# Decoding 64-bit weights: the sign kept by a parametric ReLU instead of a mask

## The chip, the cores and the metric

The kernel runs on one core of a Trainium2 chip. A core has five engines with a queue each: TensorE (matmuls, PE in the profile), VectorE (DVE), ScalarE (ACT), GpSimd (POOL) and SyncE (SP), which here sends the DMAs. Each engine works through its queue in order and waits for the others by semaphores. The time is that of one execution on the device in microseconds; before, the median of three runs is 1021.5 us.

## The reference

Attention with 32 global and 512 local positions for 8 batches of 8 heads, and behind it a feed-forward layer whose activation is h·cos(h):

```
s_g = scale * q_g @ k_all.T ; out_g = softmax(s_g) @ v_all
s_l = concat(scale * q_l @ k_g.T, where(|i-j| <= 32, scale * q_l @ k_l.T, -1e9))
out_l = softmax(s_l) @ concat(v_g, v_l)
x = concat(out_g, out_l) as (4352, 512)
h = x @ w_in            # w_in  (512, 2048), float64
out = (h * cos(h)) @ w_out   # w_out (2048, 512), float64
```

The weights come as 64-bit floats, and the kernel receives them as 64-bit words.

## The kernel before

**Staging.** Attention runs per batch b (8) and pair of heads p (4); names like `kl_0_3` or `t_0_2_1` carry b, p and, for scores, the query block. Each operand is split into a high and a low 16-bit float, and products are made of three matmuls. A pair goes: load q and k (`qkr`), maximum and scale (`qm`, `d_qk`, `pm_qk`, `qs`), split (`qa`, `kl`), copies within SBUF by DMA that rearrange halves (`kh`, `qa`, `kl`: L547 to L552), scores (`ps`, `t`), exponentials (L446), probabilities as `planes`, their transposes `pt`, and the product with v (`acc`), which becomes `xh` and `xl`. The feed-forward layer goes through chunks c of 256 rows and steps j: `ph` = x·w_in (L919), `u` and `w` (cosine by the Sin table), `gf`, its split `gh` and `gl`, and `po` = g·w_out (L975 to L977).

**Weights.** w_in comes in 8 slices `wi0` to `wi7` of 128 x 1024 words, w_out in 16 slices `wo0` to `wo15` of 128 x 512. A slice is loaded, its maximum found (L288), and later decoded and split into two 16-bit floats (`split_w`: the high part a cast on ScalarE, L281; the low part a subtraction on GpSimd, L231). w_out is loaded once for its maximum (`raw_wm`) and once more to be decoded (L416, L244). The slots are few: `wi4` and `wi5` go into the slots that `wi0` and `wi1` leave when they are decoded, and the shifted w_out words `z` have one buffer, so that the next shift waits for the cast and the subtraction of the one before.

**A decode.** The high 32-bit word of a 64-bit float, read as a 32-bit float, is scaled on ScalarE by a power of two so that a left shift by three drops the sign and the two exponent bits that are then of no use (L262, L237: `y`). VectorE makes `lo`, the bits to be put in: the top three bits of the low word with a sticky one (L263, on 16-bit words), and the sign bit in the upper half (L266, on 16-bit words). VectorE then shifts `y` and puts `lo` in (L268).

**Order.** The code gives each step a slot and a phase, and from them a priority; a scheduler with a time model of its own then sets the order in each engine's queue. A step that gets shorter in that model can move others in all queues. Attention of batches 0 and 1 and all weight decodes lie at the start of the program; later batches run beside the feed-forward layer.

Of the kernel before, what the change touches and what calls it, by code (L numbers as in the profile page):

```python
# [10 lines left out]
F32 = mybir.dt.float32  # L11
U16 = mybir.dt.uint16
I64 = mybir.dt.int64
U32 = mybir.dt.uint32
AF = mybir.ActivationFunctionType
ALU = mybir.AluOpType
# [48 lines left out]
YE = [1, 1]  # L65
# [72 lines left out]
def body(tc, qk, v, wi, wo, mask, out):  # L138
    nc = tc.nc
# [4 lines left out]
    with ExitStack() as ctx:  # L144
# [88 lines left out]
        def scaled(engine, o, a, s):  # L233
            if engine == 0:
                nc.vector.tensor_scalar(o, a, s, None, op0=ALU.mult)
            elif engine == 1:
                nc.scalar.activation(o, a, AF.Identity, scale=s)  # L237
            else:
                sb = bass.AP(tensor=s.tensor, offset=s.offset, ap=[s.ap[0]] + [(0, n) for _, n in a.ap[1:]])
                nc.gpsimd.tensor_tensor(o, a, sb, op=ALU.mult)  # L240
# [6 lines left out]
        def decode(raw, s, name, wo=0, inplace=False):  # L247

            rf, rh = raw.bitcast(F32), raw.bitcast(U16)
            n = raw.shape[-1]
            if wo:
                y = w2.tile([P, n], F32, tag="wy", name=f"y_{name}")
                lo = w2.tile([P, n], U32, tag="wlo", name=f"lo_{name}", bufs=1)
            else:
                y = w2.tile([P, n], F32, tag="raw", name=f"y_{name}")
                lo = w1.tile([P, n], U32, tag="wl1", name=f"lo_{name}")  # L260
            lh = lo.bitcast(U16)
            scaled(YE[wo], y, rf[:, 1::2], s)  # L262
            nc.vector.tensor_scalar(  # L263
                lh[:, 0::2], rh[:, 1::4], 13, 1, op0=ALU.logical_shift_right, op1=ALU.bitwise_or
            )
            nc.vector.tensor_scalar(lh[:, 1::2], rh[:, 3::4], 0x8000, None, op0=ALU.bitwise_and)  # L266
            z = w2.tile([P, n], F32, tag="wfo", name=f"z_{name}", bufs=1) if wo and not inplace else y
            zins[name] = nc.vector.scalar_tensor_tensor(  # L268
                z.bitcast(U32), y.bitcast(U32), 3, lo,
                op0=ALU.logical_shift_left, op1=ALU.bitwise_or,  # L270
            ).ins
            return z
# [78 lines left out]
        def w_in_piece(k):  # L351
            kc, c = k // 2, slice(k % 2 * 1024, k % 2 * 1024 + 1024)
            z = decode(wfs.pop(("raw", k)), wfs["s", kc], f"wi{k}")
            split_w(wi_h[:, kc, c], wi_l[:, kc, c], z)
# [63 lines left out]
        def w_out_piece(j):  # L418

            if j == 0:  # L420
                zs = [decode(slot_of(k), wsc, f"wo{k}", 1, True) for k in range(2)]
                for k in range(2):
                    split_w(wo_h[:, k], wo_l[:, k], zs[k], k < WLV)
            elif j > 1:
                raw = slot_of(j) if j < 8 else load_raw(wo[j * P : (j + 1) * P, :], f"wo{j}")
                split_w(wo_h[:, j], wo_l[:, j], decode(raw, wsc, f"wo{j}", 1), j % 4 < WLV)
# [687 lines left out]
        for c in range(NC + 1):  # L1114
            at(NS * c, -11, chunk_scales, c)
            for j in range(NS):
                s = NS * c + j
# [91 lines left out]
```

## Time and profile before

| | before |
|---|---|
| time, median of three runs (lowest, highest) | 1021.5 us (1018.31, 1022.91) |
| profiled execution, span from the first to the last instruction | 1016.1 us |
| mean granted clock of TensorE | 0.975 |
| busy: TensorE | 880.3 us (87%) |
| busy: VectorE | 712.2 us (70%), 1811 instructions |
| busy: ScalarE | 718.5 us (71%) |
| busy: GpSimd | 461.4 us (45%) |
| moved by DMA | 120.19 MB |

For the profiled execution the profile gives the span alone; it lies below the lowest of the three timed runs, which also hold what lies around the span. Busy shares are means over the whole program. The start, where weights are decoded, and the rest have different limits and are read apart below. DMA shares are the mean busy share of the core's 16 DMA engines.

### The profile page before, as it was taken

The page shows a single profiled execution, that of the slowest core. Times are in us where ns is not written, and L with a number is a line of the kernel's source. Part 1 is how long each engine was busy: PE and PEld are TensorE (multiplying, and loading weights), DVE is VectorE, ACT ScalarE, POOL GpSimd, SP SyncE. Part 2 cuts the span into 40 slices and gives each one's busy share as a digit, 9 for nine tenths or more (in the row PEclk, how much of TensorE's full clock was granted, in tenths as well). Part 3 has the DMA queues.
Part 4 walks back from the last instruction along what each step waited for, and adds up shares of the span by engine and source line. Part 5 has one row for each costly group of instructions (what it writes and reads, how often), then busy time and mean ns, then how long its engine had stood idle before and what let it go on. Part 6 is the DMA issues. An engine that isn't in the chain of part 4 may idle for free.

```text
span 1016.1 us, 21123 instructions
## 1 busy us (share of the span) xinstructions
PE 880.3 (87%) x7947; PEld 603.6 (59%) x7947; DVE 712.2 (70%) x1811; ACT 718.5 (71%) x1469; POOL 461.4 (45%) x492
## 2 busy tenths in 40 slices
PE   1245697789899998999899999998989999999996
PEld 0133565456566666566567666666666667666663
DVE  5999878995878777777787878777776865432231
ACT  5788888986678777776777767876877876534341
POOL 3696478894233333343334333432423343444442
PEclk9997899899999999999999999999999999999998
DMA  9797155766454545456554553636446452000000
GB/s 358 283 281 277 15 155 146 169 162 149 109 108 104 102 139 111 101 105 164 104 113 105 141 127 77 129 78 160 88 109 106 109 84 62 16 21 22 1 21 21
DMA packets 165823, 120.19 MB, mean 118 GB/s; under 512 B 143065, under 2 KB 143065, under 8 KB 163673
## 3 DMA queue, kind: packets, MB, share of 16 engines
q1 hardware_dynamic: 165720, 118.85, 46.8%
q8 instruction: 62, 1.02, 0.4%
q14 instruction: 41, 0.33, 0.1%
HBM read 56.00 MB, written 8.91 MB: 64 GB/s over the span
## 4 chain that ended last, share of the span: by engine, by line
PE 29%; DVE 29%; DMA 16%; ACT 14%; issue 7%; POOL 4%; SPq 1%; ACTq 0%; DVEq 0%; POOLq 0%
PE ph L919 12%; DMA qkr<-qk 9%; PE po L975 5%; PE po L977 5%; PE po L976 5%; DVE planes L705 5%; DVE t L623 4%; DMA vr<-v 4%; ACT planes L702 3%; DVE u L942 3%; DVE kl L538 3%; ACT L446 3%; DVE qm L497 2%; ACT t L446 2%; POOL w L954 2%
## 5 line engine op out<-in xcount | busy, mean ns | idle before, releaser
L919 PE MATMUL ph<-xh,wi_h 128*128 128x256 f16 x1024 | 280.8, 275 | 13.7 <-DVE gf L956 13.7
L919 PE MATMUL ph<-xh,wi_l 128*128 128x256 f16 x1024 | 281.4, 275 | 0.0
L919 PE MATMUL ph<-xl,wi_h 128*128 128x256 f16 x1024 | 281.3, 275 | 0.0
L961 POOL TENSOR_TENSOR gl<-gf,gh 128x512 f16<-128x512 f32 x136 | 166.4, 1229 | 235.7 <-ACT gh L960 235.7
L954 POOL TENSOR_TENSOR w<-w 128x512 f32<-128x512 f32 x136 | 142.5, 1051 | 249.0 <-ACT w L446 249.0
L919 PEld LDWEIGHTS <-wi_h 128*128 128x128 f16 x2176 | 211.0, 98 | 58.5 <-issue 20.4
L975 PE MATMUL po<-wo_h,gh 128*128 128x512 f16 x544 | 206.4, 381 | 17.5 <-DVE o L983 17.5
L976 PE MATMUL po<-wo_l,gh 128*128 128x512 f16 x544 | 207.1, 381 | 2.1 <-POOL wo_l L231 2.1
L977 PE MATMUL po<-wo_h,gl 128*128 128x512 f16 x544 | 206.1, 380 | 0.3 <-POOL gl L961 0.3
L446 ACT ACTIVATE w<-u,ca 128x512 f32<-128x512 f32 x136 | 97.7, 721 | 108.9 <-DVE u L942 108.4
L942 DVE SCALAR_TENSOR_TENSOR u<-u,cm,ph 128x512 f32<-128x512 f32 x136 | 100.6, 741 | 88.1 <-ACT u L941 88.1
L446 ACT ACTIVATE t<-t,mn 128x192 f32<-128x192 f32 (+1 forms) x256 | 117.0, 458 | 48.8 <-DVE mn L623 48.1
L956 DVE SCALAR_TENSOR_TENSOR gf<-w,ph 128x512 f32<-128x512 f32 x136 | 92.6, 681 | 57.3 <-POOL w L954 57.1
L960 ACT CAST gh<-gf 128x512 f16<-128x512 f32 x136 | 83.1, 611 | 67.6 <-DVE gf L956 66.7
L919 PEld LDWEIGHTS <-wi_l 128*128 128x128 f16 x1088 | 107.3, 99 | 14.6 <-issue 1.2
L623 DVE CUSTOM_DVE_ANT_0 t<-ps,msk,al 128x192 f32<-128x192 f32 (+1 forms) x256 | 99.2, 425 | 7.0 <-PE ps L607 6.8
L941 ACT ACTIVATE u<-ph,cm 128x512 f32<-128x512 f32 x136 | 92.0, 677 | 13.3 <-PE ph L919 13.2
L705 DVE SCALAR_TENSOR_TENSOR planes<-t,sm,planes 128x192 f16<-128x192 f32 (+1 forms) x200 | 87.7, 487 | 10.8 <-ACT planes L702 10.8
L976 PEld LDWEIGHTS <-gh 128*128 128x128 f16 x544 | 53.3, 98 | 69.3 <-issue 20.8
L977 PEld LDWEIGHTS <-gl 128*128 128x128 f16 x544 | 53.4, 98 | 67.1 <-issue 3.2
L975 PEld LDWEIGHTS <-gh 128*128 128x128 f16 x544 | 53.2, 98 | 49.8 <-issue 0.9
L702 ACT ACTIVATE planes<-t,sm 128x192 f16<-128x192 f32 (+1 forms) x200 | 75.6, 454 | 0.0
(184 smaller groups left out, 1415.0 us busy)
## 6 DMA issues: line engine op xcount, KB each, us to landing
qkr<-qk SPq DMA_DIRECT2D x29, 608.0 KB, 4.9
vr<-v SPq DMA_DIRECT2D x8, 1280.0 KB, 8.4
kh<-qa SPq DMA_DIRECT2D x62, 152.0 KB, 2.6
out<-o SPq DMA_DIRECT2D x34, 256.0 KB, 3.2
raw_wm<-wo SPq DMA_DIRECT2D x16, 512.0 KB, 7.8
qa<-kl SPq DMA_DIRECT2D x31, 152.0 KB, 3.9
kl<-kl SPq DMA_DIRECT2D x31, 152.0 KB, 4.4
wo_h<-wi SPq DMA_DIRECT2D x4, 1024.0 KB, 6.9
```

What stands on the lines that cost most here:

```text
L446: ins = nc.scalar.activation(*a, **k).ins
L623: nc.vector.tensor_tensor_reduce(t[:, h], pt[:, h], msk[:, MOFF[i] : MOFF[i] + w], al, 3.0e38, ALU.add, ALU.min, mn[:, h : h + 1],)
L702: nc.scalar.activation(hi, t[:, h], AF.Identity, scale=r)
L705: nc.vector.scalar_tensor_tensor(lo, t[:, h], r, hi, op0=ALU.mult, op1=ALU.subtract)
L919: nc.tensor.matmul(ph[:, a], w[:, kc, f], x[:, kc, q], start=first and ip == 0, stop=last and ip == 2, skip_group_check=True,)
L942: nc.vector.scalar_tensor_tensor(u, u, m, ph, op0=ALU.subtract, op1=ALU.subtract)
L954: nc.gpsimd.tensor_tensor(w, w, w, op=ALU.mult)
L956: nc.vector.scalar_tensor_tensor(gf, w, 0.5, st.pop(("ph", c, j)).rearrange("p a b -> p (a b)"), op0=ALU.subtract, op1=ALU.mult,)
L961: nc.gpsimd.tensor_tensor(gl, gf, gh, op=ALU.subtract)
L975: nc.tensor.matmul(po[k], gh[:, q], wo_h[:, f], start=(f == 0), stop=False)
L976: nc.tensor.matmul(po[k], gh[:, q], wo_l[:, f], start=False, stop=False)
L977: nc.tensor.matmul(po[k], gl[:, q], wo_h[:, f], start=False, stop=(f == NJ - 1))
```

## The change

ScalarE's scaling becomes a Prelu with the same scale and a slope of 2^32 for negative values. A negative word thereby gets 32 more in its exponent field, and the left shift by three carries that bit, the sixth of the exponent, into the place of the sign. So `lo` has no sign to hold: one VectorE instruction on whole 32-bit words makes it, and the mask is gone.

```
-            rf, rh = raw.bitcast(F32), raw.bitcast(U16)
+            rf = raw.bitcast(F32)
...
-            lh = lo.bitcast(U16)
-            scaled(YE[wo], y, rf[:, 1::2], s)
+            nc.scalar.activation(y, rf[:, 1::2], AF.Prelu, scale=s, alpha=2.0**32)
             nc.vector.tensor_scalar(
-                lh[:, 0::2], rh[:, 1::4], 13, 1, op0=ALU.logical_shift_right, op1=ALU.bitwise_or
-            )
-            nc.vector.tensor_scalar(lh[:, 1::2], rh[:, 3::4], 0x8000, None, op0=ALU.bitwise_and)
+                lo, raw.bitcast(U32)[:, 0::2], 29, 1, op0=ALU.logical_shift_right, op1=ALU.bitwise_or
+            )
```

Each of the 24 decodes loses one VectorE instruction (1813 become 1789); the counts on the other engines stay, with 58 loads of an activation table in both. In the new kernel all lines behind the edit have numbers lower by two, so that its L266 is the old L268, and its L262 is the new instruction. The scheduler also sets another order in the early part of every queue: the last 1294 instructions on VectorE, 890 on ScalarE, 13307 on TensorE, 257 on GpSimd and 258 on SyncE stand as before.

The first place is VectorE at the second pair of w_in slices (`y_wi0` is the shift of slice 0, `lo_wi2` the bits of slice 2, `ws3_2` the maximum of slice 4, `gt` the global scores, L288 before and L286 now the maximum). Before:

```order
L268 SCALAR_TENSOR_TENSOR y_wi1_242<-y_wi1_242,lo_wi1_243 128x1024
L263 TENSOR_SCALAR lo_wi2_361<-raw_wi2_186 128x1024
L266 TENSOR_SCALAR lo_wi2_361<-raw_wi2_186 128x1024
L815 ISA gt_0_0_309,gmn_0_0_310<-gps_0_0_0_300,zero_74,gal_0_0_311 128x288
L815 ISA gmn_0_0_310 128x1
L263 TENSOR_SCALAR lo_wi3_440<-raw_wi3_188 128x1024
L266 TENSOR_SCALAR lo_wi3_440<-raw_wi3_188 128x1024
L623 ISA t_0_1_0_386,mn_0_1_0_387<-ps_0_1_0_381,msk_73,al_0_1_162 128x192
```

Now:

```order
L266 SCALAR_TENSOR_TENSOR y_wi1_241<-y_wi1_241,lo_wi1_242 128x1024
L262 TENSOR_SCALAR lo_wi2_359<-raw_wi2_185 128x1024
L343 TENSOR_SCALAR wm43_1_351<-wim_107 128x1
L262 TENSOR_SCALAR lo_wi3_437<-raw_wi3_187 128x1024
L301 TENSOR_SCALAR ws_1_350<-wm43_1_351 128x1
L196 TENSOR_SCALAR wie_108<-wm43_1_351 128x1
L302 TENSOR_SCALAR ws_1_350<-ws_1_350 128x1
L309 TENSOR_SCALAR pw_i_90<-wie_108 128x1
L286 TENSOR_REDUCE ws3_2_424<-wo_h_88 128x1
L310 TENSOR_SCALAR pw_i_90<-pw_i_90 128x1
L813 ISA gt_0_0_307,gmn_0_0_308<-gps_0_0_0_298,zero_74,gal_0_0_309 128x288
```

Two instructions of the pair are gone, and the maximum of slice 4 stands ahead of the scores, which it followed before.

The second place is SyncE's queue at the last copy of batch 0 (`kl_0_3`; `raw_wm` are w_out slices for the maximum, `vr_1` is v of batch 1). Before:

```order
L416 DMA wo_l_89<-wo 128x512
L407 DMA raw_wm2_254<-wo 128x512
L552 DMA kl_0_3_326<-kl_0_3_326 64x1216
L464 DMA vr_1_1160<-v 128x2560
L407 DMA raw_wm3_257<-wo 128x512
L244 DMA raw_wo8_1754<-wo 128x512
```

Now:

```order
L414 DMA wo_l_89<-wo 128x512
L462 DMA vr_1_1152<-v 128x2560
L405 DMA raw_wm3_255<-wo 128x512
L550 DMA kl_0_3_324<-kl_0_3_324 64x1216
L244 DMA raw_wo8_1738<-wo 128x512
```

The copy moved behind the load of v and the last load for the maximum.

The third place is ScalarE at the exponentials of pair 3 (`t_0_3`), with the transposed probabilities of pair 2 (`pt_0_2`), the copies of v (`vh_1_0`) and the first w_out slices (`y_wo0`). Before:

```order
L495 ACTIVATE kl_1_0_1448,qm_1_0_1447<-qkr_1_0_1408 128x1216
L446 ACTIVATE t_0_3_0_590,sm_0_3_833<-t_0_3_0_590,mn_0_3_0_591 128x192 x2
L561 ACTIVATE vh_1_0_1314,vm4_1_1313<-vr_1_1160 128x640
L446 ACTIVATE t_0_3_1_599,sm_0_3_833<-t_0_3_1_599,mn_0_3_1_600 128x224 x2
L446 ACTIVATE t_0_3_2_608,sm_0_3_833<-t_0_3_2_608,mn_0_3_2_609 128x224 x2
L715 COPY pt_0_2_931<-tr_0_2_1_942 128x1024
L446 ACTIVATE t_0_3_3_617,sm_0_3_833<-t_0_3_3_617,mn_0_3_3_618 128x192 x2
L446 ACTIVATE gt_0_1_505,gsm_0_1_842<-gt_0_1_505,gmn_0_1_506 128x544
L715 COPY pt_0_2_931<-tr_0_2_3_962 128x1024
L702 ACTIVATE planes0_76<-t_0_3_0_590,sm_0_3_833 128x192 x2
```

Now:

```order
L713 COPY pt_0_2_924<-tr_0_2_1_935 128x1024
L559 ACTIVATE vh_1_0_1306,vm4_1_1305<-vr_1_1152 128x640
L713 COPY pt_0_2_924<-tr_0_2_3_955 128x1024
L493 ACTIVATE kl_1_0_1438,qm_1_0_1437<-qkr_1_0_1398 128x1216
L444 ACTIVATE t_0_3_0_585,sm_0_3_827<-t_0_3_0_585,mn_0_3_0_586 128x192 x2
L444 ACTIVATE t_0_3_1_594,sm_0_3_827<-t_0_3_1_594,mn_0_3_1_595 128x224 x2
L444 ACTIVATE t_0_3_2_603,sm_0_3_827<-t_0_3_2_603,mn_0_3_2_604 128x224 x2
L444 ACTIVATE t_0_3_3_612,sm_0_3_827<-t_0_3_3_612,mn_0_3_3_613 128x192 x2
L444 ACTIVATE gt_0_1_501,gsm_0_1_836<-gt_0_1_501,gmn_0_1_502 128x544
L261 ACTIVATE y_wo0_1382<-wo_h_88,wsc_111 128x512
L773 ACTIVATE xh_0_1134<-acc_0_2_1017,xs_91 128x512
L261 ACTIVATE y_wo1_1387<-wo_l_89,wsc_111 128x512
```

The copies moved ahead of the exponentials, and the scaling of the first two w_out slices, which stood behind the planes, moved ahead of them. Behind the planes the casts of these two slices (L279, before L281) now stand ahead of both `pt_0_3` copies; before, one of the copies came first.

## Prediction

> **What bounds the kernel now.** I read the page's span and slices first, to see where each engine is full:
>
> ```profile
> span 1016.1 us, 21123 instructions
> ...
> DVE  5999878995878777777787878777776865432231
> ACT  5788888986678777776777767876877876534341
> ```
>
> A digit is a slice of 25.4 us. VectorE is full in the second to fourth slice, with ScalarE close to it; both ease off only at the end. Then the stretches (start and end; busy time and count of TensorE, weight loads, VectorE, ScalarE, GpSimd; granted clock; DMA share; GB/s), cut where the kernel changes character:
>
> ```profile
> 18.00:65.00 47.00, 16.59 (x110) 11.00 (x110) 46.35 (x122) 36.18 (x75) 30.06 (x42) 1.00 0.85 295
> 65.00:90.00 25.00, 9.50 (x104) 7.04 (x106) 24.76 (x71) 17.86 (x37) 21.45 (x29) 0.81 1.01 317
> 90.00:126.00 36.00, 25.72 (x359) 19.63 (x353) 30.72 (x82) 32.40 (x68) 18.44 (x27) 0.83 0.22 67
> 126.00:245.00 119.00, 100.61 (x908) 67.50 (x908) 97.00 (x253) 102.24 (x210) 96.11 (x126) 0.95 0.61 149
> 245.00:1016.00 771.00, 727.40 (x6473) 498.25 (x6470) 507.89 (x1266) 518.82 (x1068) 286.27 (x253) 0.99 0.41 93
> ```
>
> From 18 to 65 us VectorE works 46.35 of 47.00 us: it is the limit, with the DMA at 0.85 close behind. From 65 to 90 VectorE (24.76 of 25.00) and the DMA (1.01) are both full. From 90 to 245 nothing is: VectorE, ScalarE, GpSimd and TensorE all work some 80%, and wait for each other in queue order. From 245 us TensorE works 727.40 of 771.00 us. All 24 decodes lie before 245 us, and in the tail every engine's order is the same in both kernels. So the tail should keep its length, and what counts is when it starts.
>
> The chain that ended last (start, length, what), over the start of the program, goes through decode instructions:
>
> ```profile
> 20.32 0.62 DVE lo_wi L266
> ...
> 26.24 0.62 DVE lo_wi L266
> ```
>
> **The change part by part.** *Removed:* the second instruction of each decode, L266 of the old kernel. Its busy time by stretch (then clock, DMA share, GB/s), and its sum:
>
> ```profile
> 18.00:65.00 47.00, 6.09 (x6) 1.00 0.85 295
> 65.00:90.00 25.00, 2.49 (x3) 0.81 1.01 317
> 90.00:126.00 36.00, 4.59 (x7) 0.83 0.22 67
> 126.00:245.00 119.00, 6.38 (x8) 0.95 0.61 149
> ...
> sum 998.00, DVE 19.55; mean DVE 3.91
> ```
>
> *Replaced on VectorE:* the first instruction (L263, 16-bit words read at a stride of 8 bytes) becomes one on 32-bit words at the same stride. The trace has no such instruction. The nearest rows (ns min/median/max) are L263 itself and the 32-bit shift with two inputs, L268:
>
> ```profile
> L263 DVE TENSOR_SCALAR lo_wo<-raw_wo x8: 458/735/1086, 130.7 to 200.1; 128x512 uint16<-128x512 uint16 x8
> L263 DVE TENSOR_SCALAR lo_wi<-wo_h x4: 731/801/871, 19.6 to 55.7; 128x1024 uint16<-128x1024 uint16 x4
> L268 DVE SCALAR_TENSOR_TENSOR y_wi<-y_wi,lo_wi x8: 1205/1214/1679, 31.8 to 84.3; 128x1024 uint32<-128x1024 uint32 x8
> ```
>
> For 1024 elements that bounds it between 0.73 us and 1.21 us. I take L263's own durations, since one input of equal stride and count is the nearer form; so 19.55 us of VectorE work go. At the upper end each of the eight w_in decodes costs 1.21 − 0.80 = 0.41 us more, and the gain of the first stretch (six of them) falls by 2.5 us.
>
> [...]
>
> *Replaced on ScalarE:* 24 Identity become 24 Prelu, with the same strided input and the same scale operand; alpha is a constant. No Prelu is in the trace. Rows (busy, mean ns, idle before it):
>
> ```profile
> L237 ACT ACTIVATE y_wo<-raw_wo,wsc 128x512 f32<-128x512 f32 x8 | 6.1, 757 | 0.8 <-DMA raw_wo<-wo 0.8
> L281 ACT CAST wo_h<-z_wo 128x512 f16<-128x512 f32 x14 | 8.5, 608 | 1.6 <-DVE z_wo L268 1.6
> L446 ACT ACT_TABLE_LOAD x57 | 73.1, 1283 | 1.5 <-DVE u L942 0.5
> ```
>
> Between a cast without scale (608) and an Identity followed by a table load (757 + 1283) I take 757, the same operands. Loads aren't added: the order shows 58 of them in both kernels. So this part costs nothing; if each Prelu did need a load, 24 x 1.283 = 30.8 us would come onto ScalarE, and that is the far end.
>
> *First stretch.* 6.09 us go from the engine that is the limit. But its output is mostly permission for the next load: SyncE stood in front of the w_in loads, waiting for the scaled words (in total, times, longest):
>
> ```profile
> SPq L327 <- ACT y_wi L237: 11.3, 4, 7.8
> ```
>
> The first load request can come earlier only by the two L266 ahead of it, 0.62 + 0.62 = 1.24 us; and the order now has VectorE take the maximum of that load's data ahead of the scores, so it will stand and wait for it. Bounds for what passes on into the full DMA after 65 us are 1.24 and 6.09; I take **−2.5**, twice the lower end, since only the later requests gain more. The 2.49 us of the second stretch I cost at **0**: there the DMA at 1.01 covers them.
>
> *The moved copy.* SyncE's queue now sends the copy kl_0_3 (L552) behind the v load of batch 1 and the last raw_wm load. Issues, then landings:
>
> ```profile
> 78.79 0.48 SPq L552 DMA_DIRECT2D kl<-kl  x1
> 80.13 0.34 SPq L464 DMA_DIRECT2D vr<-v  x1
> 81.57 0.33 SPq L407 DMA_DIRECT2D raw_wm<-wo  x1
> ```
> ```profile
> kl<-kl SPq DMA_DIRECT2D x1, 152.0 KB, 11.0
> raw_wm<-wo SPq DMA_DIRECT2D x1, 512.0 KB, 12.4
> PE gps L794 <- DMA kl<-kl: 6.9, 2, 5.5
> ```
>
> The copy landed at 78.79 + 11.0 = 89.8 and TensorE had stood 5.5 us for it. The load that will be ahead of it landed at 81.57 + 12.4 = 94.0. So the copy comes **+4.2** later, before the −2.5.
>
> *ScalarE's queue after it.* Two pt copies and one vh go from among the exponentials of pair 3 to ahead of them, where ScalarE waits anyway; one pt copy goes behind the two wo_h casts that start the w_out chain. From the chain and ScalarE's order of time:
>
> ```profile
> 93.61 0.72 ACT vh L561 x2
> ...
> 96.19 0.89 ACT pt L715
> ...
> 104.99 0.89 ACT pt L715
> ```
> ```profile
> 112.23 0.67 ACT L775 ACTIVATE xh<-acc,xs 128x512 f16<-128x512 f32 x1
> ...
> 118.06 1.24 ACT L941 ACTIVATE u<-ph,cm 128x512 f32<-128x512 f32 x2
> ```
>
> That is 0.72 + 2 x 0.89 = **−2.5**, and **−0.9** for the last. Against it y_wo0, y_wo1 and xh now stand before the planes, 2 x 0.757 + 0.67 = 2.2 us; that delays pair 3's last xh, not the casts, and xh (112.23) is covered by the 5.8 us until u (118.06), which stands behind the w_out chain. If the cover went, 2.2 us would come back.
>
> *90 to 245 us.* The 4.59 us in the third stretch lie beside that w_out chain (cast, GpSimd, shift, one buffer): **0**. In the fourth VectorE is 97.00 of 119 us busy and no part is the limit. The page's chain gives:
>
> ```profile
> PE 29%; DVE 29%; DMA 16%; ACT 14%; issue 7%; POOL 4%; SPq 1%; ACTq 0%; DVEq 0%; POOLq 0%
> ```
>
> Bounds are 0, if every removed instruction there had a wait of another engine beside it, and 6.38. I take VectorE's share: 0.29 x 6.38 = **−1.9**.
>
> Sum: −2.5 + 4.2 − 2.5 − 0.9 − 1.9 = −3.6 us. The profiled execution would go from 1016.1 to 1012.5; what lies around its span, 1021.5 − 1016.1 = 5.4 us against the median of the three runs, stays. **Forecast 1021.5 − 3.6 = 1017.9 us.**
>
> **The rivals.**
>
> *Full gain.* The later requests draw all loads forward, so that the removed work counts wherever VectorE is full: 6.09 + 2.49 = 8.6, and 0.29 x (4.59 + 6.38) = 3.2 behind it: 1021.5 − 11.8 = 1009.7 us. For it: 46.35 of 47.00. Against it: the DMA share of 1.01 right behind, and the moved copy.
>
> *Late copy (slower).* The requests gain nothing, the copy lands at 94.0 or later, and ScalarE's three pieces do not help, because the vh ahead of the exponentials reads the very v load that is in front of the copy (80.13 plus its own landing). Then +4.2 stands alone: 1025.7 us. It decides if the copy lands later than 89.8 + 2.5 = 92.3 us. For it: TensorE's 5.5 us wait shows that nothing covers this copy. Against: VectorE's lead should bring the queue forward.
>
> *Nothing left.* Copy and gains cancel, and the rest hides behind the DMA: 1021.5 us.
>
> *It costs more than it says.* The 32-bit instruction at L268's price or Prelu dearer than Identity: 2.5 us of the gain go, 1020.4 us.
>
> **How the numbers follow.** Forecast 0.42 (its own range 1014 to 1021), full gain 0.24, late copy 0.17, nothing left 0.10, dearer instructions 0.07. About 0.5%, 5.1 us, is what a measurement of this kernel can tell from no change: faster means below 1016.4, slower above 1026.6. Full gain lies below, and a quarter of the forecast's range: 0.36. Above are half of the late copy and a little of the others, since a queue order can also cost in the fourth stretch: 0.12. The rest, 0.52, is within. The range runs from just under full gain to just over the late copy, 1008.5 to 1026.5; the runs of before alone differ by 4.6 us.
>
> **What would show it.** L266's row gone, and the new row (L262) near 0.8 us for 1024 elements; near 1.2 the fourth rival is right. Prelu at 757 ns and 58 table loads. VectorE idle before the maximum of the fifth w_in slice, where there was no idle. The copy kl_0_3 landing between 90 and 92.3 us: the forecast; at 94, the late copy; below 88, full gain. The first u (L941) near 116.3 instead of 118.06. From the first shared instruction of the tail to the end as long as now; if the tail's own length moves by over 2 us, the argument that only its start counts is wrong.

## The result, and the profile after

| | before | after |
|---|---|---|
| time, median of 15 runs each, beside each other | 1020.84 us | 1025.27 us |
| ratio after/before | | 1.005, 95% interval 1.0032 to 1.0068 |
| profiled execution, span | 1016.1 us | 1021.2 us |
| busy, VectorE | 712.2 us | 695.8 us |

The kernel is slower by half a per cent, about 5.1 us. 1017.9 us was forecast, with the range up to 1026.5. In three of the experiments below one run took over 1800 us; medians and ratios leave it out. VectorE has 16.4 us less to do and the kernel ends later, so the question is what took up the time that was freed.

First the new instructions: the one that makes `lo` (count, shortest/median/longest ns), the Prelu and the table loads (busy us, mean ns).

```profile
L262 DVE TENSOR_SCALAR lo_wo<-raw_wo x8: 410/613/778, 132.3 to 200.8; 128x512 uint32<-128x512 uint32 x8
L262 DVE TENSOR_SCALAR lo_wi<-wo_h x4: 682/684/1075, 19.5 to 55.5; 128x1024 uint32<-128x1024 uint32 x4
L262 DVE TENSOR_SCALAR lo_wi<-raw_wi x4: 687/885/1102, 32.8 to 76.0; 128x1024 uint32<-128x1024 uint32 x4
```
```profile
L444 ACT ACT_TABLE_LOAD x57 | 73.1, 1283 | 1.0
L261 ACT ACTIVATE y_wo<-raw_wo,wsc 128x512 f32<-128x512 f32 x8 | 6.1, 761 | 1.5 <-DMA raw_wo<-wo 1.5
```

Both cost what was forecast: 0.68 to 0.89 us at the median for 1024 elements, and 761 ns for a Prelu where the Identity took 757, with no load added. The instructions aren't the reason.

The stretches of the new kernel, columns as in the prediction:

```profile
18.00:65.00 47.00, 15.60 (x121) 10.95 (x121) 44.23 (x125) 37.94 (x78) 29.86 (x44) 0.78 0.91 313
65.00:90.00 25.00, 9.20 (x91) 6.63 (x91) 20.05 (x60) 16.14 (x35) 18.59 (x29) 0.64 0.97 338
90.00:126.00 36.00, 26.64 (x356) 20.24 (x355) 23.96 (x69) 29.19 (x60) 15.34 (x24) 0.74 0.13 28
126.00:245.00 119.00, 98.42 (x821) 65.94 (x821) 90.79 (x238) 100.72 (x207) 97.01 (x127) 0.94 0.63 147
245.00:1016.00 771.00, 729.43 (x6561) 500.43 (x6558) 511.18 (x1277) 522.02 (x1077) 287.85 (x254) 0.99 0.42 93
```

VectorE, full before between 65 and 90 us (24.76), now works 20.05 of 25.00: the time was freed, and it stands idle. Two places where the new order makes an engine stand show on other queues. The first is SyncE between 24 and 32 us, and with it TensorE at pair 1's scores (start, us, what; in brackets the idle time before and its releaser). Before, the copy `kl_0_1` was sent first:

```profile
29.64 0.47 SPq L552 DMA_DIRECT2D kl<-kl  x1
31.77 1.46 SPq L327 DMA_DIRECT2D wo_h<-wi  x2
```
```profile
31.98 0.40 PE L794 MATMUL gps<-kl,qa 128*32 128x288 f16 x1 [1.39 <-DMA kl<-kl]
```

After:

```profile
30.44 0.33 SPq L325 DMA_DIRECT2D wo_h<-wi  x1
30.86 0.47 SPq L550 DMA_DIRECT2D kl<-kl  x1
```
```profile
36.93 0.40 PE L792 MATMUL gps<-kl,qa 128*32 128x288 f16 x1 [7.15 <-DMA kl<-kl]
```

The load of the fifth w_in slice (1 MB, into the slot that slice 0 left) is now sent ahead of the small copy `kl_0_1` (152 KB), and TensorE stands 7.15 us for that copy, which lands 6.0 us after it was sent at 30.86. The second is the place where pair 3's scores begin. Before, on TensorE:

```profile
89.86 0.40 PE L794 MATMUL gps<-kl,qa 128*32 128x288 f16 x1 [5.47 <-DMA kl<-kl]
```

After, on TensorE and on GpSimd:

```profile
89.54 0.86 PE L712 MATMUL tr<-ident,planes 128*128 128x128 f16 x6 [10.43 <-ACT planes L691]
92.39 0.96 PE L712 MATMUL tr<-ident,planes 128*128 128x128 f16 x6 [1.99 <-POOL planes L693]
94.44 1.65 PE L712 MATMUL tr<-ident,planes 128*128 128x128 f16 x14 [1.10 <-ACT pt L713]
96.03 0.42 PE L792 MATMUL gps<-kl,qa 128*32 128x288 f16 x1
```
```profile
84.74 2.55 POOL L231 TENSOR_TENSOR wi_l<-y_wi,wi_h 128x256 f16<-128x256 f32 x4 [5.09 <-ACT wi_h L279]
87.25 2.01 POOL L683 TENSOR_TENSOR t<-t,sm 128x192 f32<-128x192 f32 x4
89.21 2.55 POOL L231 TENSOR_TENSOR wi_l<-y_wi,wi_h 128x256 f16<-128x256 f32 x4
91.72 4.33 POOL L693 TENSOR_TENSOR planes<-t,planes 128x224 f16<-128x224 f32 x8
```

26 of pair 2's 32 transposes (`tr`) now stand ahead of the second part of the global scores (`gps`, the first instruction that needs `kl_0_3`) and of pair 3's scores. They wait for the planes. The first of them are made on ScalarE (L691) from the softmax that GpSimd works on until 89.26 us (`t`, L683), the next on GpSimd itself (L693); both steps of GpSimd stand behind low parts of w_in. So pair 3's scores begin at 96.03 us; before, at 89.86. The first `u` follows:

```profile
120.89 1.34 ACT L939 ACTIVATE u<-ph,cm 128x512 f32<-128x512 f32 x2 [0.17 <-PE ph L917]
```

That is 2.8 us later than the 118.06 of before. At the start of the tail the distance is 3.6 us (a `u` that ended at 244.75 ends at 248.33).

### The profile page after: what moved, and what is told of

It reads as the page before. It is cut to its first block, busy times and chain, and to the rows that moved or that the text cites. A ratio compares the mean times of both kernels' runs of the same rounds, so it can differ in the third digit from the quotient of the medians.

```text
span 1021.2 us, 21096 instructions
## 1 busy us (share of the span) xinstructions
PE 879.8 (86%) x7947; PEld 604.4 (59%) x7947; DVE 695.8 (68%) x1787; ACT 717.0 (70%) x1469; POOL 457.8 (45%) x492
## 4 chain that ended last, share of the span: by engine, by line
PE 32%; DVE 23%; DMA 12%; ACT 12%; POOL 6%; issue 5%; SPq 1%; ACTq 0%; DVEq 0%; POOLq 0%
PE ph L917 14%; DMA qkr<-qk 8%; DVE planes L703 5%; PE po L973 5%; PE po L974 5%; PE po L975 5%; DVE t L621 3%; DVE u L940 3%; ACT planes L700 3%; ACT t L444 3%; POOL w L952 2%; DVE qm L495 2%; DMA vr<-v 2%; DVE kl L536 2%; ACT L444 2%
## 5 line engine op out<-in xcount | busy, mean ns | idle before, releaser
L939 ACT ACTIVATE u<-ph,cm 128x512 f32<-128x512 f32 x136 | 92.3, 679 | 14.6 <-PE ph L917 14.6
L703 DVE SCALAR_TENSOR_TENSOR planes<-t,sm,planes 128x192 f16<-128x192 f32 (+1 forms) x200 | 88.2, 490 | 10.4 <-ACT planes L700 10.4
```

The source lines that it names most:

```text
L703: nc.vector.scalar_tensor_tensor(lo, t[:, h], r, hi, op0=ALU.mult, op1=ALU.subtract)
```

## The experiments

Two things changed at once: the instructions, and through the scheduler the order of five queues. Each experiment is the new kernel (or the old one) with an order held or one constraint added. An order is held by a chain of dependencies without semaphores, from a table of numbers:

```
+        held = {"P": "83 84 121+3 ...", "A": "...", "D": "...", "G": "...", "S": "..."}
+        emitted = list(nc.cur_bb.bb.instructions)
+        for runs in held.values():
+            ...
+            for i, j in zip(seq, seq[1:]):
+                tc.add_manual_dep(emitted[j], emitted[i].name, order, reason="program_order")
```

The results, each beside runs of the kernel before on the same chip. The last three columns are read from one profile of each kernel, in us: the first matmul that needs `kl_0_1`, the first that needs `kl_0_3`, and the end of the first `u`, all counted so that the first w_in maximum ends at 19.60 (in most profiles it does within 0.3; in e3 and e11 all that comes early is 1.9 and 2.3 us later).

| kernel | median us | ratio to before (95%) | pair 1's scores | pair 3's scores | first u |
|---|---|---|---|---|---|
| before | 1020.8 | 1 | 31.9 | 89.8 | 118.7 |
| after | 1025.3 | 1.0050 (1.0032 to 1.0068) | 36.9 | 96.0 | 121.6 |
| e1 new instructions, old order | 1010.0 | 0.9899 (0.9877 to 0.9921) | 31.8 | 84.4 | 112.7 |
| e2 old instructions, new order | 1028.9 | 1.0092 (1.0060 to 1.0125) | 38.0 | 99.5 | 126.0 |
| e3 after, scores first | 1022.3 | 1.0008 (0.9990 to 1.0026) | 37.2 | 93.8 | 118.6 |
| e4 after, kl_0_3 ahead | 1024.9 | 1.0032 (1.0012 to 1.0052) | 36.8 | 96.1 | 122.2 |
| e5 after, kl_0_1 ahead, rest free | 1016.9 | 0.9967 (0.9950 to 0.9985) | 31.9 | 83.9 | 119.5 |
| e6 after, kl_0_1 ahead, rest held | 1023.2 | 1.0023 (0.9997 to 1.0049) | 31.7 | 94.5 | 119.5 |
| e7 e1 with kl_0_1 late | 1015.9 | 0.9968 (0.9949 to 0.9987) | 37.4 | 87.7 | 116.3 |
| e8 e1 with transposes first | 1019.6 | 1.0002 (0.9983 to 1.0021) | 31.2 | 92.2 | 120.1 |
| e9 e1 with kl_0_3 late | 1018.0 | 0.9966 (0.9944 to 0.9988) | 32.2 | 88.7 | 116.6 |
| e10 e1 with kl_0_3 early | 1014.2 | 0.9912 (0.9882 to 0.9942) | 32.0 | 81.9 | 115.8 |
| e11 e1, new decode for w_in alone | 1016.6 | 0.9945 (0.9926 to 0.9965) | 32.0 | 86.3 | 115.2 |
| e12 e1 with e7's and e8's swaps | 1020.3 | 1.0016 (0.9999 to 1.0033) | 37.1 | 95.6 | 123.6 |

**e1 and e2: instructions and order apart.** e1 is the new kernel with the table of the order of before for all five queues; e2 is the old kernel with the table of the order of after, each mask right behind its first instruction.

> The new decode instructions, but all five queues hold the order of the kernel before (2157 instructions of the first 245 us are chained in it). Theory ORDER (the new order of TensorE's queue, which transposes pair 2's planes ahead of pair 3's scores, costs the time; the shorter decode alone saves some): 1016 to 1019 us, faster than before's 1020.8 by 2 to 5 us; pair 3's scores start near 90 us as before, the first u ends at or before 118.7 us. Theory INSTRUCTION (the new instructions themselves, by what they do beside other engines or to the granted clock, cost it): about 1025 us as after. Theory COPY (only the late copy kl_0_3 costs): 1018 to 1021, since the copy too is back in its old place; this run doesn't tell COPY from ORDER.

> The old decode (Identity, two 16-bit instructions, 37.2 us of them), but all five queues hold the order of the kernel after. ORDER: no better than after's 1025.3 us, 1025 to 1030, since the order costs and nothing is saved. INSTRUCTION: near before's 1020.8 us.

e1 took 0.9899 of before, a gain of 10 us where 2 to 5 were expected; e2 took 1.0092. So the instructions alone gain 1.0% in the old order, and the order alone costs 0.9% with the old instructions (1.5% with the new: 1.0050 less 0.9899). The instruction theory is out. The places in e1, with TensorE, SyncE and ScalarE's first `u`:

```profile
31.81 0.40 PE L792 MATMUL gps<-kl,qa 128*32 128x288 f16 x1 [1.41 <-DMA kl<-kl]
...
84.42 0.40 PE L792 MATMUL gps<-kl,qa 128*32 128x288 f16 x1 [6.54 <-DMA kl<-kl]
```
```profile
29.44 0.47 SPq L550 DMA_DIRECT2D kl<-kl  x1
30.44 1.45 SPq L325 DMA_DIRECT2D wo_h<-wi  x2
```
```profile
112.00 1.25 ACT L939 ACTIVATE u<-ph,cm 128x512 f32<-128x512 f32 x2
```

Here the copy leaves ahead of the load and lands 2.3 us after its issue, against 6.0 us behind it. Up to 30 us the instructions of VectorE, ScalarE and GpSimd that take over 0.55 us end within 0.04 us of each other in the profiles of e1 and after; the two part at this copy.

**e3 and e4: the two waits ahead of pair 3's scores.** e3 adds one dependency to the new kernel and leaves the rest to the scheduler; e4 holds the new order and moves one DMA.

In the diff, `t` is a transpose and `lastsc` the last score matmul of a pair; below it stands the exchange in e4's table for SyncE.

```
-                    nc.tensor.transpose(tr[:, k], pl[:, k * P : (k + 1) * P], ident16)
+                    t = nc.tensor.transpose(tr[:, k], pl[:, k * P : (k + 1) * P], ident16).ins
+                    if p == 2: tc.add_manual_dep(t, st["lastsc", 0, 3].name, order, reason="program_order")
```
```
-vr_1, raw_wm15, kl_0_3
+kl_0_3, vr_1, raw_wm15
```

> The kernel after with one order added on TensorE: pair 2's transposes stand behind pair 3's scores; the scheduler is free with the rest. It still sends the copy kl_0_3 behind the v load of batch 1. ORDER: pair 3's scores start when the copy has landed, near 91 us instead of 96.0; the first u ends 3 to 5 us before after's 121.6; 1018 to 1022 us. COPY: the copy lands at 91 as in after, 1024 to 1026 us. INSTRUCTION: 1024 to 1026 us.

> The kernel after in exactly its own order, but for one DMA: the copy kl_0_3 is sent ahead of the v load of batch 1 and the last raw_wm load. It lands 4 to 11 us earlier than after's 91.0 us. COPY: 1019 to 1022 us. ORDER: nothing changes, 1024.5 to 1026 us, since TensorE stands at pair 2's transposes until 96.0 us, behind the landed copy. INSTRUCTION: 1024.5 to 1026 us.

e4 changed nothing that can be told from after (1.0032 against 1.0050, the intervals overlap): TensorE still stood at the transposes until 96.1. The copy got away only 1.8 us earlier than in after, and landed near 88.2 instead of 91.0, less than expected; its wait was covered already. e3 took the transposes away, and TensorE then waited for the copy:

```profile
95.71 0.40 PE L793 MATMUL gps<-kl,qa 128*32 128x288 f16 x1 [14.30 <-DMA kl<-kl]
```

95.71 less the 1.9 us by which this profile starts later is 93.8: the 94.0 that the prediction gave the late copy. So two waits lie side by side here, and to take one away shows the other. e3's first `u` comes 3.0 us before after's, the low end of what was expected, and it gained 0.4%.

**e5 and e6: the first copy, in the new kernel.** e5 adds one dependency and leaves the rest free; e6 holds the new order and moves this one DMA.

The line of e5, and the exchange in e6's table for SyncE:

```
+        tc.add_manual_dep(loads[4].ins, st["copy", 0, 1].name, order, reason="program_order")
```
```
-load wi4, kl_0_1, load wi5
+kl_0_1, load wi4, load wi5
```

> The kernel after with one order added on SyncE: the load of the fifth w_in slice stands behind the copy kl_0_1 (pair 1 of batch 0); the scheduler is free with the rest, and now puts pair 3's scores ahead of pair 2's transposes by itself. In the kernel after this copy stood behind that load and landed at 36.9 us instead of 31.8. Theory COPY1 (the loss begins there; all that differs between 35 and 120 us follows from it): 1010 to 1014 us, first u near 112.7 us as in e1. Theory LATE ORDER (most of it comes from the order behind 85 us): 1018 to 1022 us, since only the scores' place changes there as in e3.

> The kernel after in exactly its own order, but for one DMA: the copy kl_0_1 is sent ahead of the load of the fifth w_in slice. Theory BARE (the transfer's lateness alone costs): pair 1's scores start near 32 us, everything behind is 4 us earlier, 1019 to 1022 us. Theory BUILT AROUND (the other queues were set in order for the late copy: VectorE takes the maximum of that slice ahead of the minima of the scores, ScalarE waits in queue order): at most 1.2 us, 1023.5 to 1025.5 us.

e6 moved pair 1's scores from 36.9 to 31.7, and only 2.0 us of that reached the first `u`. The reason stands on VectorE, in the order that was set around the late copy:

```profile
35.62 1.22 DVE L286 TENSOR_REDUCE ws<-wo_h 128x1 f32<-128x1024 f32 x1 [0.40 <-DMA wo_h<-wi]
```

The maximum of the fifth slice stands ahead of the scores' minima, so VectorE waits for the load that is now behind the copy. e6 is nearer to "built around", though its 1023.2 us lie just below that range. In e5 the scheduler drops both mistakes by itself and gains 0.8% on after, the best of the free orders, between the two expectations; but the first `u` comes at 119.5, not 112.7, so its order costs in another place. One place that differs is VectorE at pair 2: it takes the minima of that pair's scores from 78.5 us on, in e1 from 66.2. GpSimd then stands 4.5 us at that pair's softmax (`t`, L683), until 89.7 us; in e1 it starts there at 83.0. The view names `wm_o` as the releaser, which ends within 0.1 us of the reciprocals of the pair's sums. No run changes this place alone.

```profile
POOL t L683 <- DVE wm_o L429: 4.5, 1, 4.5
```

**e7, e8, e9, e12: each swap by itself, put into e1.** The table of e1 with one exchange each:

```
e7  SyncE:   -kl_0_1, load wi4              +load wi4, kl_0_1
e8  TensorE: -gps_1, ps_3_0, tr_2 ...       +24 of tr_2, gps_1, ps_3_0 ...
e9  SyncE:   -kl_0_3, vr_1, raw_wm15        +vr_1, raw_wm15, kl_0_3
e12 e7 and e8
```

> The kernel of e1 (new instructions, order of before), but for one DMA: the load of the fifth w_in slice is sent ahead of the copy kl_0_1, as in the kernel after. COPY1: pair 1's scores start near 36.9 us instead of 31.8, VectorE and ScalarE stand behind them, 1013 to 1016 us. Rival (something else covers it): within 1 us of e1's 1010.0.

> The kernel of e1, but TensorE transposes three of pair 2's four tiles (24 of 32) ahead of pair 3's scores, as the kernel after does. Theory TRANSPOSES (the scores now wait for GpSimd's planes, near 92 us in e1): pair 3's scores start 3 to 4 us later, 1013 to 1015 us. Rival (the wait is covered, as the copy kl_0_3 lands late too): 1010 to 1011 us.

> The kernel of e1, but the copy kl_0_3 is sent behind the v load of batch 1 and the last raw_wm load, as in the kernel after. Theory COPY3 COUNTS (nothing covers this copy where the scores stand first on TensorE): in e1 it landed at 84.4 us and TensorE had waited 6.5 us; 1.79 MB more ahead of it at 355 GB/s make it 3 to 5 us later, 1012 to 1015 us. Rival (covered here too, as e4 showed it to be in the new order): 1009 to 1011 us.

> The kernel of e1 with both of the swaps of e7 and e8 (the load of the fifth w_in slice ahead of the copy kl_0_1; 24 of pair 2's transposes ahead of pair 3's scores), all else in the order of before. Theory TWO SWAPS (they are what the new order costs): the first u ends 9 to 11 us later than e1's 112.7, the time comes near that of the kernel after, 1022 to 1027 us. Rival (they share one wait, and the rest of the new order costs as well): first u 7 to 8 us later as in e8 alone, 1018 to 1021 us.

TensorE in e7, in e8 and in e9:

```profile
37.60 0.40 PE L792 MATMUL gps<-kl,qa 128*32 128x288 f16 x1 [8.08 <-DMA kl<-kl]
```
```profile
85.50 0.86 PE L712 MATMUL tr<-ident,planes 128*128 128x128 f16 x6 [7.73 <-ACT planes L691]
88.02 0.96 PE L712 MATMUL tr<-ident,planes 128*128 128x128 f16 x6 [1.66 <-POOL planes L693]
...
92.06 0.42 PE L792 MATMUL gps<-kl,qa 128*32 128x288 f16 x1
```
```profile
88.70 0.40 PE L792 MATMUL gps<-kl,qa 128*32 128x288 f16 x1 [10.84 <-DMA kl<-kl]
```

Each swap costs by itself: e7 0.7% of the time (0.9968 less 0.9899), as expected, and 3.6 us at the first `u`; e8 1.0% and 7.4 us, about twice what was expected; e9 0.7% and 3.9 us, with the landing in the expected place and more time than expected. e12 has the first two: at the first `u` they add up (3.6 and 7.4 us, together 10.9), in time it costs 1.2% where the sum is 1.7%, with about 0.2% of interval to either side of each ratio. With these two its first `u` is even 2.0 us later than in the kernel after, so they are enough for the whole delay there. With e9's 3.9 us the sum would be larger than what after shows, so the three do not all count in after at once (e4 shows it for the third). In time e12 stays 0.34% below after, with intervals that just touch. That the rest of the new order costs as well can't be read from this: at the start of the tail e12 is still over 0.6 us later than after, and only its tail, which has the same order, is 4.9 us shorter in its one profile. This difference stays open. Of e12's two theories the first is right on the mechanism, and the rival on the time.

**e10 and e11: what else e1's order holds.** e10 sends `qa_0_3` ahead of the w_out loads at 63 us and `kl_0_3` ahead of six of them; e11 is e1 with the old decode for w_out.

```
e10 SyncE:  -raw_wm x3, qa_0_3, raw_wm, wo x6, raw_wm, kl_0_3     +qa_0_3, raw_wm x4, kl_0_3, wo x6, raw_wm
e11 decode: +if wo: (the old three lines)  else: (the new two)
```

> The kernel of e1, but the two copies qa_0_3 and kl_0_3 are sent ahead of the w_out loads that fill the queue from 63 us. Theory COPY3 COUNTS: kl_0_3 lands near 76 us instead of 84.4, pair 3's scores start at 78 to 82; ScalarE reaches their exponentials at 87 us in e1 with almost no wait ahead of them, so only 1 to 3 us are left: 1007 to 1009 us. Rival (ScalarE's and VectorE's own work sets pair 3's softmax, or the delayed maxima of w_out give it back): 1009 to 1012 us.

> The kernel of e1, but the 16 w_out decodes are the old ones (Identity, two 16-bit instructions); only the 8 w_in decodes are new. The first u was 6.1 us earlier in e1 than before, and 8.0 at the start of the tail. Theory WI FIRST (the full VectorE of the first 85 us carries the gain): first u 4 to 6 us earlier than before, 1012 to 1015 us. Rival WO (the chain cast, GpSimd, shift of w_out behind 100 us carries it): first u under 3 us earlier, 1016 to 1019 us.

e10 gained nothing (0.9912 against 0.9899), and its 1014.2 us lie above both expectations: pair 3's scores begin 2.5 us earlier, but the loads behind it are later, VectorE waits 3.4 us for `raw_wm`, and the first `u` loses 3.2 us. e11 keeps 0.55% of the 1.01%: its first `u` is 3.5 us earlier than before, between the two expectations, with a time in the rival's range, and e1's another 2.5 us. Both decodes carry the gain, about half each.

## Why the prediction was wrong

The forecast was 1017.9 us, a gain of 3.6; measured was a loss of 5.1. That lies inside the stated range, but the time moved the other way. What failed is how the new order was priced: the exchange of a load and `kl_0_1` on SyncE and the move of the transposes on TensorE are not in the sum, and their counterpart on ScalarE stands in it as a gain of 2.5 us. By its steps:

*What bounds the kernel; the instructions.* Right. The durations came out a little under those taken: on 1024 elements L262 has medians of 0.684 us (`wo_h`) and 0.885 (`raw_wi`), where L263 had 0.801 and 0.930 (its row for `raw_wi` before: 768/930/1158 ns); the shortest took 0.682, the longest 1.102. With the order held, the rival "full gain" was right in its number: it said 1009.7 us, and e1 took 1010.0. Its parts fit less well: e1's profile is 8.0 us ahead at the start of the tail, where the rival has 11.8.

*First stretch, −2.5; 65 to 126 us, 0 and 0; 126 to 245 us, −1.9.* The w_in decodes bring 3.5 us to the first `u` (e11), a little above the term. The w_out decodes between 90 and 126 us were costed at nothing, beside the chain of cast, GpSimd and shift; they bring 2.5 us (e1 against e11). By the start of the tail another 1.9 us is gained in e1: a `u` that ended at 244.75 ends there 8.0 us earlier, and the first `u` 6.1. That is the forecast's 1.9 in size; in e11, with the old w_out decodes, this part gains nothing (3.2 us there against 3.5 at the first `u`). That VectorE's share of the chain is the right measure for it is not shown.

*The moved copy kl_0_3, +4.2.* Right in size: 3.9 us at the first `u` in e9, and 93.8 us for its landing in e3. In the new kernel it landed at 91.0, only 1.2 us later than before, and didn't count, since the transposes ahead of it waited longer (e4). The sign that the prediction gave for its forecast, a landing between 90 and 92.3 us, came; the forecast was wrong all the same, since that sign looks at the copy alone. The rival "late copy" said 1025.7 us, next to the 1025.3 measured. That is luck: the copy landed before the 92.3 us that were its condition, and in e4, with the copy sent earlier, nothing was gained.

*ScalarE's pieces, −2.5.* This step failed, with its sign. That `pt_0_2` now stood ahead of pair 3's exponentials was taken for a gain on ScalarE, since ScalarE waits there. The same move on TensorE's queue, the transposes ahead of pair 3's scores, is not in the prediction. It makes the scores wait for GpSimd's planes: 7.4 us at the first `u` in e8. What ScalarE's own exchanges are worth, the −2.5, the −0.9 and the 2.2 against them, no run shows by itself.

*The step that is not in the sum.* The prediction says that the first load request can come earlier only by the two masks ahead of it, 1.24 us. It came 1.33 us earlier (30.44 instead of 31.77). That alone does not bring it past the copy `kl_0_1`, which before was sent at 29.64: in e1 the load leaves at the same 30.44, and the copy ahead of it at 29.44. It was the scheduler that put the load in front, and in the new kernel the copy stood behind it until 30.86. The shorter decode didn't only draw a load forward; through the order, the load took the place ahead of a transfer that TensorE was waiting for. The prediction follows SyncE's queue at `kl_0_3` alone; the same kind of exchange 48 us earlier is not in it. It costs 3.6 us at the first `u` and 0.7% (e7).

*The tail.* From the `u` at 244.75 (248.33 after) to the end of the span the length grows by 1.5 us (771.4 to 772.9), within the 2 us allowed. In the twelve experiments it lies between 767.8 and 776.0 us with the tail's order as good as unchanged, so a difference of a few us there in one profile says nothing.

The account at the first `u`: −6.0 us by the instructions (e1), +8.9 us by the order, together the +2.9 measured. In time −10 and +15 us; e7, e8 and e9 cost some 3 us more in time than at the first `u`. Of that, 0.6 to 1.8 us are there at the start of the tail; the rest stays open, with about 2 us of interval to either side of each ratio.

## What to carry to other kernels

Where a scheduler sets the order, the removal of an instruction is two changes; the second can be larger than the first, and to hold the old order is a way to get the gain alone (0.9899 here, the fastest of all fourteen kernels). In a comparison of two orders, take each small transfer or short step that an engine stands and waits for in the old profile, and look it up in the new queue, on the queue that issues it and on the one that waits; look for large loads and long waits that have come in front. Two waits that lie side by side can hide each other, so that the cure of one alone shows little (nothing in e4, 0.4% in e3).

## What the runs showed of the hardware

In the profile after, the granted clock of TensorE is 0.78 from 18 to 65 us and 0.64 from 65 to 90. e4 has the same instructions in the same order, but for one DMA behind 75 us, and was granted more in both stretches:

```profile
18.00:65.00 47.00, 15.68 (x121) 10.95 (x121) 44.46 (x125) 37.95 (x78) 29.99 (x44) 1.00 0.92 312
65.00:90.00 25.00, 9.64 (x91) 7.05 (x91) 19.99 (x60) 16.04 (x35) 18.45 (x29) 0.85 0.96 322
```

TensorE's busy time is the same to 0.5 us, the first `u` is as late (122.2 against 121.6), and the times can't be told apart. The clock looked like a cause, since it was low just where the loss began; but here it differed between executions of as good as one order, and where TensorE waits most of the time (15.6 us busy of 47.0) it cost nothing that can be seen. What makes 0.78 out of 1.00, no run here shows.

A copy of 152 KB that landed 2.3 us after its issue (e1) took 6.0 us (after) behind one load of 1 MB that was sent 0.4 us earlier on the same queue; the load, too, landed 6.0 us after it was sent. In e7, which is e1 with these two exchanged, TensorE began on the copy's data 6.6 us after the copy was sent (31.01 to 37.60).
